# Tokens stored by partition and ids worked out behind the routing, in an attention kernel with expert routing

## Chip, cores and metric

The kernel runs on one core of one Trainium2 chip. The metric is device time in microseconds of one execution. The three runs of the kernel before took 408.19, 408.69 and 409.09 us, median 408.69 us.

## The reference

Attention with pairs of queries averaged, and then one of eight experts (two matrices with a ReLU between) for each token. The output of the attention, heads side by side, is the `x` of the experts.

```python
# q, k, v: 8 batches, 8 heads, 1152 positions, 64 wide
q_pool = q.reshape(B, H, S // 2, 2, D).mean(axis=3)          # 576 queries
scores = (1 / sqrt(D)) * q_pool @ k.T
attn = exp(scores - max) / (sum + 1e-09)
x = (attn @ v).transpose(0, 2, 1, 3).reshape(4608, 512)      # token = batch * 576 + query
for e in range(8):                                           # w1: 512x1024, w2: 1024x512
    mask = domain_id == e
    out[mask] = relu(x[mask] @ w1[e]) @ w2[e]
```

## The kernel before

**Attention.** The 64 heads go through in 32 pairs, four pairs a batch. Time is cut into steps `t`, 12 a pair, 384 in all (`NST`). Scores (`score`, L613) are made in groups of 504 columns for both heads of a pair, ScalarE takes the exponential of a group (`expo`, L621), and TensorE multiplies it with v (`av`, L633). The product of a head gathers in one PSUM bank, `acc`, of which there is one only. When nine chunks are in it, `evac` (L646, L648) takes the reciprocal of the sums and writes the normalised 64 columns of that head into `xb`, on VectorE; until then TensorE can't begin the next head's product. `xb` holds a batch: 128 partitions, five row groups `i`, 512 columns; two such buffers take turns. Row group 0 has 64 rows of its own, the others 128 each, together 576 queries.

A table written out by hand (`PLAN`) says what TensorE does between two score groups: `A` is a product, `P` a piece of an expert's tile, `K` a filler. TensorE's order does not depend on times.

**Stores and gathers.** `put_x` writes a row group of a finished batch to `x_tok` in DRAM in token order. A token's row depends on the query's place in blocks of 96 (`QP`), so a batch is cut into nine stores of 32 to 96 rows (`CUT`), one row group a step behind the batch's last evacuation (`put`). The stores of the first seven batches stand on SyncE's queue, those of the last take turns on SyncE and GpSimd. `get_x` marks a buffer `xs` on VectorE (L96) and then gathers 128 rows of one expert from `x_tok` on GpSimd (L675). Tiles 0 to 2 of an expert hold only rows of the first 2, 4 and 6 batches, tiles 3 and 4 need all.

**Routing.** While attention runs, VectorE works out, from a list `rq` with a cost for each step, which token goes to which slot of which expert: one-hot tables, counts, a running sum, the slot of each token (`rt_...`). `rt_tok` computes the token number that belongs to each partition and row group. Then numbers are moved into slot order with matmuls (`id_...`): `id_prep` splits token number plus one into two digits, `id_group` and `id_lo` make one-hot tiles, `id_mm` (L474) multiplies five of them at a time, two steps behind the last of them (`mmq`), and `id_end` puts the digits together: `grow` (row of `x_tok`, for the gathers) and `gid` (row of the output, for the scatters). Three more steps (`extra`) follow for slots beyond an expert's room.

**Experts.** 14 tiles are worked off as `P` pieces inside attention; the rest comes behind it, expert by expert: `stage1` (L1073), `turn_tile` (L1092: transposes of a gathered tile), `stage2` (L1120), and a scatter of each finished tile.

## Time and profile before

| | |
|---|---|
| median of three runs | 408.69 us |
| the profiled execution | 407.95 us |
| its span (first to last instruction) | 405.9 us |
| busy: TensorE, ScalarE, VectorE, GpSimd | 381.2, 329.3, 230.2, 182.1 us |
| last exponential ends, last matmul of the experts ends (about) | 306.5, 397.7 us |
| granted TensorE clock | 1.00 in nearly the whole span |

Busy time is the union of an engine's records. Records of one engine may overlap, since an instruction can start before the one ahead of it has left the engine. "xb" or "acc" in a row is the tile that is written, what follows "<-" is read. A number in square brackets at the end of a row is idle time of that engine just before, with what seems to have ended it.

### The profile page before, as it was taken

What the parts mean: (1) busy time and instruction counts of PE and PEld (TensorE: products, weight loads), DVE (VectorE), ACT (ScalarE), POOL (GpSimd) and SP (SyncE); (2) the same over time, 40 slices, a digit from 0 to 9 for tenths busy, and PEclk for the clock granted to TensorE, in tenths of its full rate; (3) what the DMA queues carried; (4) which work ended last, traced back from release to release, by engine and by line L of the source; (5) the groups of instructions that cost most, each with busy time, mean ns of one, the idle gap of its engine ahead of it and who ended that gap; (6) DMA issues with size and microseconds to landing.
All of it is one profiled execution on the core that took longest, in us unless ns stands there. A gap on an engine that the chain in (4) does not pass through costs nothing.

```text
span 405.9 us, 14850 instructions
## 1 busy us (share of the span) xinstructions
PE 381.2 (94%) x6341; PEld 259.5 (64%) x6341; DVE 230.2 (57%) x638; ACT 329.3 (81%) x396; POOL 182.1 (45%) x303
## 2 busy tenths in 40 slices
PE   8889888988999999999999999999999999999992
PEld 5456555655676766766767676776776677765542
DVE  4488789985555666555766575566544235433231
ACT  4999999999999999999999999999993333423220
POOL 4633222321645555043433343743443884772522
PEclk9999999999999999999999999999999999999998
DMA  8999999995999999989878865969993399699902
GB/s 216 210 226 236 225 244 236 228 227 125 188 227 250 263 222 232 241 195 255 192 164 191 173 124 126 245 129 211 131 204 90 96 148 209 198 135 167 253 26 100
DMA packets 52751, 76.70 MB, mean 189 GB/s; under 512 B 12239, under 2 KB 41456, under 8 KB 52674
## 3 DMA queue, kind: packets, MB, share of 16 engines
q0 software_dynamic: 38208, 66.53, 80.6%
q1 hardware_dynamic: 14194, 8.99, 10.7%
q8 instruction: 51, 0.84, 0.9%
q14 instruction: 26, 0.21, 0.2%
q10 hardware_dynamic: 272, 0.13, 0.1%
HBM read 95.20 MB, written 14.68 MB: 271 GB/s over the span
## 4 chain that ended last, share of the span: by engine, by line
PE 72%; ACT 12%; DVE 7%; DMA 3%; issue 3%; SPq 1%; POOL 0%; POOLq 0%; ACTq 0%; DVEq 0%
PE s L613 17%; PE acc L633 16%; ACT er L621 12%; PE op L1120 11%; PE hp L1073 10%; PE px L822 6%; PE px L809 6%; DMA q<-in_q_dram 3%; PE s L579 2%; DVE kq L584 2%; DVE xb L648 1%; DVE qz L589 1%; PE px L788 1%; SPq L664 1%; PE hp L1092 1%
## 5 line engine op out<-in xcount | busy, mean ns | idle before, releaser
L621 ACT ACTIVATE er<-s 128x1008 f16<-128x1008 f32 x330 | 298.2, 1110 | 1.1 <-PE s L613 0.8
L633 PE MATMUL acc<-v,er 128*128 128x65 f16 x2835 | 117.4, 194 | 7.4 <-DVE xb L648 4.4
L633 PEld LDWEIGHTS <-er 128*128 128x128 f16 x2880 | 99.9, 97 | 36.6 <-issue 18.3
L613 PE MATMUL s<-qz,kq 64*128 64x504 f16 (+6 forms) x1152 | 112.6, 286 | 6.2 <-ACT er L621 2.7
L675 POOL DMA_INDIRECT xs<-x_tok,grow x40 | 40.7, 1016 | 87.1 <-issue 19.6
L528 POOL DMA_INDIRECT out_dram<-osb,gid x40 | 41.4, 1035 | 62.4 <-DVE osb L828 32.5
L613 PEld LDWEIGHTS <-kq 64*128 64x128 f16 x1152 | 44.1, 94 | 38.5 <-issue 21.0
L117 POOL DMA_DIRECT2D vs<-in_v_dram x32 | 24.0, 749 | 50.1 <-DVE v L554 16.2
L1120 PE MATMUL op<-w2h,hT 128*128 128x512 f16 (+1 forms) x200 | 45.8, 379 | 0.0
L1073 PEld LDWEIGHTS <-w1h 128*128 128x128 f16 x384 | 32.6, 98 | 12.1 <-issue 0.5
L1126 ACT COPY osb<-op 128x512 f32<-128x512 f32 (+1 forms) x14 | 8.2, 583 | 37.8 <-PE op L1120 37.8
L1073 PE MATMUL hp<-xt,w1h 128*128 128x224 f16 (+3 forms) x352 | 38.6, 268 | 0.2 <-ACT hT L1078 0.2
L1080 DVE TENSOR_SCALAR hT<-hp 128x224 f16<-128x224 f32 (+3 forms) x40 | 19.1, 477 | 33.2 <-PE hp L1073 27.1
L1078 ACT ACTIVATE hT<-hp 128x224 f16<-128x224 f32 (+3 forms) x40 | 17.0, 427 | 21.9 <-PE hp L1073 21.6
L584 DVE COPY kq<-s 128x1152 f16<-128x1152 f16 x31 | 23.4, 756 | 18.2 <-PE s L579 15.3
L1120 PEld LDWEIGHTS <-hT 128*128 128x128 f16 (+1 forms) x200 | 20.1, 105 | 18.9
L646 DVE RECIPROCAL cum<-acc 128x5 f32<-128x5 f32 x47 | 9.0, 192 | 40.9 <-PE acc L633 40.7
L809 PE MATMUL px<-xt,w1h 128*128 128x128 f16 x448 | 30.8, 219 | 0.0
L822 PE MATMUL px<-w2h,h 128*128 128x512 f16 x112 | 30.2, 381 | 0.0
L544 DVE TENSOR_TENSOR qp<-q 96x768 f16<-96x768 f32 x31 | 29.3, 946 | 1.4 <-DMA q<-in_q_dram 1.3
L809 PEld LDWEIGHTS <-w1h 128*128 128x128 f16 x448 | 25.3, 98 | 4.9 <-issue 4.7
L814 DVE TENSOR_SCALAR h<-px 128x512 f16<-128x512 f32 x28 | 19.3, 690 | 15.2 <-PE px L809 15.1
(150 smaller groups left out, 346.1 us busy)
## 6 DMA issues: line engine op xcount, KB each, us to landing
q<-in_q_dram POOLq DMA_DIRECT2D x28, 576.0 KB, 8.1
vs<-in_v_dram POOLq DMA_DIRECT2D x32, 288.0 KB, 6.9
k<-in_k_dram POOLq DMA_DIRECT2D x31, 288.0 KB, 6.7
w1h<-in_moe_w_dram POOLq DMA_DIRECT2D x16, 512.0 KB, 13.2
w2h<-in_moe_w_dram POOLq DMA_DIRECT2D x16, 512.0 KB, 13.0
x_tok<-xb SPq DMA_DIRECT2D x23, 96.0 KB, 5.5
q<-in_q_dram SPq DMA_DIRECT2D x3, 576.0 KB, 5.3
x_tok<-xb SPq DMA_DIRECT2D x23, 64.0 KB, 5.4
```

The costliest lines, as they stand in the source:

```text
L117: nc.gpsimd.dma_start(vs[:, :, :, :], v[b, h : h + 2].rearrange("h (p c) d -> p h c d", p=P))
L528: ins = nc.gpsimd.indirect_dma_start(out=dst[:, :], out_offset=bass.IndirectOffsetOnAxis(ap=ap, axis=0), in_=src, in_offset=None, **kw,)
L544: nc.vector.tensor_tensor(out=qp[0:QP, :, :, :].rearrange("p j h d -> p h j d"), in0=q2[:, :, :, 0:D], in1=q2[:, :, :, D : 2 * D], op=ALU.add,
L584: nc.vector.tensor_copy(kq[p][:, :].rearrange("p (c r k) -> p r c k", c=NC, r=2), mt[:, :, 0 : NC * 64].rearrange("p r (c k) -> p r c k", ...
L613: nc.tensor.matmul(s[:, r, o : o + n], lhsT=kq[p][lo:hi, c * P : (c + 1) * P], rhs=qz[p % 2][lo:hi, q0 : q0 + n], start=True, stop=True,)
L621: nc.scalar.activation(er[:, :, o : o + w], st.pop(k)[:, :, 0:w], AF.Exp, bias=0.0, scale=0.0625)
L633: nc.tensor.matmul(acc[p, h][:, i * (D + 1) : (i + 1) * (D + 1)], lhsT=er[:, h, o : o + P], rhs=v16[p % NV][:, c, h, 0 : D + 1], start=c = ...
L675: nc.gpsimd.indirect_dma_start(out=dst, out_offset=None, in_=x_dram[0 : 1 + nb * Sp, :], in_offset=bass.IndirectOffsetOnAxis(ap=ap, axis=0),)
L809: nc.tensor.matmul(m[:, f % 4, :], lhsT=wts[e][0][:, cc, f * P : (f + 1) * P], rhs=h0["xt"][:, cc, :], start=cc == 0, stop=cc == ND - 1,)
L822: nc.tensor.matmul(h0["o"][:, :], lhsT=h0["h"][:, f, :], rhs=wts[e][1][:, f, :], start=f == 0, stop=f == NF - 1,)
L1073: nc.tensor.matmul(hp_[:, lo : lo + n], lhsT=w1h[:, cc, f * P : (f + 1) * P], rhs=xt[:, cc, lo : lo + n], start=cc == 0, stop=cc == ND - 1,)
L1120: nc.tensor.matmul(op_[0:r, :], lhsT=hT[:, f, i * P : i * P + r], rhs=w2h[:, f, :], start=f == 0, stop=f == NF - 1,)
```

## The change

`x_tok` gets a row for each partition and row group: row 1 + b * 640 + 5 * p + i. A batch of `xb` then lies in DRAM as 128 pieces of 5 KB, one for each partition, and goes out in one store, right behind its last evacuation. Rows 64 to 127 of row group 0 are written too and read by nobody, so `x_tok` has 5121 rows instead of 4609. The last batch goes in two parts: columns 0 to 383 behind pair 30, columns 384 to 511 behind pair 31, each part in two halves of 64 partitions, on SyncE and GpSimd.

The routing moves row numbers instead of token numbers, which are an iota (`row1`), so `rt_tok` goes. `grow` comes out of `id_end` as before. The token number `gid` is worked out from the row behind that, in six steps (`id_tok`), with three divisions with rounding. A gather waits for `id_end` (`ready`) and no longer for the list to be empty. The id matmuls come three steps behind their tiles instead of two. Pieces of a tile that is begun when attention's last step comes are done ahead of the last products, with the ReLU on ScalarE. The path for experts with more tokens than room, and the one for sums out of range, are fitted to the new rows; neither runs on these inputs.

```diff
@@ sizes, tables
+    XB = NQ * P
+    NX = B * XB
-    x_dram = nc.dram_tensor("x_tok", (N + 1, Dm), F16, kind="Internal").ap()
+    x_dram = nc.dram_tensor("x_tok", (NX + 1, Dm), F16, kind="Internal").ap()
-    pos = perm.tile([P, B, NQ], I32, name="pos")
-    nc.gpsimd.iota(pos[:, :, :], pattern=[[0, B], [P, NQ]], base=-64, channel_multiplier=1)
-    nc.gpsimd.iota(pos[:, :, 0:1], pattern=[[0, B], [0, 1]], base=0, channel_multiplier=1)
-    bof = perm.tile([P, B, NQ], I32, name="bof")
-    nc.gpsimd.iota(bof[:, :, :], pattern=[[Sp, B], [0, NQ]], base=0, channel_multiplier=0)
+    row1 = perm.tile([P, B, NQ], I32, name="row1")
+    nc.gpsimd.iota(row1[:, :, :], pattern=[[XB, B], [1, NQ]], base=1, channel_multiplier=NQ)
-    nc.gpsimd.memset(pat[:, :], N)
+    nc.gpsimd.memset(pat[:, :], NX)
@@ the routing
-    def rt_tok(i):
...
-            tk = perm.tile([P, NT], I32, name="tk")
-            tf = tok[:, :, :].rearrange("p b i -> p (b i)")
-            nc.vector.tensor_scalar(
-                out=tk[:, :], in0=tf, scalar1=1.0, scalar2=None, op0=ALU.add
-            )
+            tk = row1[:, :, :].rearrange("p b i -> p (b i)")
@@ id_end and what follows it
         nc.vector.tensor_copy(grow[:, :], va[:, :])
-        vz = perm.tile([P, NH], FP32, name="vz")
+        gst["va"] = va
+
+    MAGIC = 12582912.0
+
+    def floor_of(dst, x, n):
+
         nc.vector.tensor_scalar(
-            out=vz[:, :], in0=va[:, :], scalar1=0.0, scalar2=float(N + 1),
-            op0=ALU.is_equal, op1=ALU.mult,
-        )
-        nc.vector.scalar_tensor_tensor(
-            out=gid[:, :], in0=va[:, :], scalar=-1.0, in1=vz[:, :], op0=ALU.add, op1=ALU.add
-        )
+            out=dst, in0=x, scalar1=1.0 / n, scalar2=0.5 - 0.5 / n, op0=ALU.mult, op1=ALU.subtract
+        )
+        nc.vector.tensor_scalar(out=dst, in0=dst, scalar1=MAGIC, scalar2=None, op0=ALU.add)
+        nc.vector.tensor_scalar(out=dst, in0=dst, scalar1=MAGIC, scalar2=None, op0=ALU.subtract)
+
+    vz, vb, vj, vp = (perm.tile([P, NH], FP32, name=n) for n in ("vz", "vb", "vj", "vp"))
+
+    def token_of(step, dst, r, bt, jt, pt):
+
+        if step == 0:
+            floor_of(bt, r, XB)
+            nc.vector.scalar_tensor_tensor(
+                out=jt, in0=bt, scalar=-float(XB), in1=r, op0=ALU.mult, op1=ALU.add
+            )
+        elif step == 1:
+            floor_of(pt, jt, NQ)
+            nc.vector.scalar_tensor_tensor(
+                out=jt, in0=pt, scalar=-float(NQ), in1=jt, op0=ALU.mult, op1=ALU.add
+            )
+        elif step == 2:
+            nc.vector.scalar_tensor_tensor(
+                out=pt, in0=jt, scalar=float(P), in1=pt, op0=ALU.mult, op1=ALU.add
+            )
+            nc.vector.tensor_scalar(
+                out=jt, in0=jt, scalar1=1.0, scalar2=-float(QO[1]), op0=ALU.is_ge, op1=ALU.mult
+            )
+            nc.vector.tensor_tensor(out=pt, in0=pt, in1=jt, op=ALU.add)
+        elif step == 3:
+            floor_of(jt, pt, QP)
+            nc.vector.tensor_scalar(out=pt, in0=pt, scalar1=float(NJ), scalar2=None, op0=ALU.mult)
+        else:
+            nc.vector.scalar_tensor_tensor(
+                out=pt, in0=bt, scalar=float(Sp), in1=pt, op0=ALU.mult, op1=ALU.add
+            )
+            nc.vector.scalar_tensor_tensor(
+                out=dst, in0=jt, scalar=-float(Sp - 1), in1=pt, op0=ALU.mult, op1=ALU.add
+            )
+
+    def id_tok(step):
+        if step == 0:
+            va = gst["va"]
+            nc.vector.tensor_scalar(
+                out=vz[:, :], in0=va[:, :], scalar1=0.0, scalar2=float(NX + 1),
+                op0=ALU.is_equal, op1=ALU.mult,
+            )
+            nc.vector.scalar_tensor_tensor(
+                out=vz[:, :], in0=va[:, :], scalar=-1.0, in1=vz[:, :], op0=ALU.add, op1=ALU.add
+            )
+        else:
+            token_of(step - 1, gid[:, :], vz[:, :], vb[:, :], vj[:, :], vp[:, :])
@@ stores and gathers
-    def put_x(b, i):
-        kept.append((b, i))
-        for lo, hi in zip(CUT, CUT[1:]):
-            i_, m = (0, lo) if lo < 64 else (1 + (lo - 64) // P, (lo - 64) % P)
-            if i_ == i:
-                j, p0 = divmod(lo, QP)
-                (ends[len(cut) % 2] if b == B - 1 else nc.sync).dma_start(
-                    x_dram[1 : N + 1, :].rearrange("(b p j) c -> b j p c", b=B, j=NJ)[
-                        b, j, p0 : p0 + hi - lo, :
-                    ],
-                    xb[b][m : m + hi - lo, i, :],
-                )
-                if b == B - 1:
-                    cut.append((b, i))
+    kept = []
+
+    def put_x(b, lo=0, hi=Dm):
+
+        rows = x_dram[1 + b * XB : 1 + (b + 1) * XB, lo:hi].rearrange("(p i) c -> p i c", i=NQ)
+        if b == B - 1:
+            for eng, p0 in ((nc.sync, 0), (nc.gpsimd, P // 2)):
+                eng.dma_start(rows[p0 : p0 + P // 2], xb[b][p0 : p0 + P // 2, :, lo:hi])
+        else:
+            nc.sync.dma_start(rows, xb[b][:, :, lo:hi])
+        if hi == Dm:
+            kept.append(b)
 
     def gather(dst, ap, nb=B):
         nc.gpsimd.memset(gap[:, :], 0.0)
         nc.gpsimd.indirect_dma_start(
-            out=dst, out_offset=None, in_=x_dram[0 : 1 + nb * Sp, :],
+            out=dst, out_offset=None, in_=x_dram[0 : 1 + nb * XB, :],
             in_offset=bass.IndirectOffsetOnAxis(ap=ap, axis=0),
         )
@@ up
-            if f % 4 == 3:
+            if f % 4 == 3 and now[0] >= NST:
+                nc.scalar.activation(h0["h"][:, f - 3 : f + 1, :], m[:, :, :], AF.Relu)
+            elif f % 4 == 3:
                 nc.vector.tensor_scalar(
                     out=h0["h"][:, f - 3 : f + 1, :], in0=m[:, :, :],
                     scalar1=0.0, scalar2=None, op0=ALU.max,
@@ product
+    CL = 2 * (HP - 1) * D
         if c == NC - 1:
             evac(p, h)
             if p % HP == HP - 1 and h == 1:
-                for i in range(NQ):
-                    if p < NPAIR - 1:
-                        put[t + 1 + i] = (p // HP, i)
-                    else:
-                        put_x(p // HP, i)
+                put_x(p // HP, 0 if p < NPAIR - 1 else CL)
+            if p == NPAIR - 2 and h == 1:
+                put_x(B - 1, 0, CL)
@@ lists
-    rq += [(330, lambda i=i: rt_tok(i)) for i in range(4)]
-            mmq.append((now[0] + 2, c - GL + 1))
+            mmq.append((now[0] + 3, c - GL + 1))
-    extra = [(330, lambda: rt_over(0)), (500, lambda: rt_over(1)), (330, lambda: rt_d(1))]
+    extra = [(330, lambda i=i: id_tok(i)) for i in range(6)]
+    extra += [(330, lambda: rt_over(0)), (500, lambda: rt_over(1)), (330, lambda: rt_d(1))]
@@ main loop
+            for _ in range(len(cur) or len(blocks[0]) if started() else 0):
+                piece()
             for h, c in lead + [(0, 7), (1, 7), (0, 8), (1, 8)]:
                 product(t, (NPAIR - 1, h, c), LAST if h else ACC)
-            while cur or blocks and len(begun) and len(blocks) % 4:
+            while started():
                 piece()
-        if main and want and t >= want[0][2] and t >= last_get + 5 and not (t in later) and not mmq and not rq:
+        if main and want and t >= want[0][2] and t >= last_get + 5 and not (t in later) and ready:
                 id_mm(mmq.pop(0)[1])
                 if not rq and not mmq:
                     id_end()
+                    ready.append(t)
                     rq, extra = extra, []
-        if t in put:
-            put_x(*put.pop(t))
```

**VectorE**, between the evacuations of pair 7, head 1, and of pair 8, head 0 (`rr` and `cum` hold reciprocals, `qp`, `v`, `kp` are the inputs of later pairs, `ov`, `ovi`, `ext`, `oaddr` belong to the routing's end). Before, from the first evacuation to the second:

```order
L648 TENSOR_TENSOR xb<-acc,rr_184 128x5x64
L324 TENSOR_SCALAR ovi<-ov 1x8
L327 TENSOR_SCALAR ovi<-ovi 1x8
L330 TENSOR_REDUCE ovm<-ov 128x1
L544 TENSOR_TENSOR qp_98<-q_1708 96x2x6x64
L349 TENSOR_SCALAR ext<-ext 128x40
L353 TENSOR_TENSOR ext<-ext,isov 128x40
L354 TENSOR_SCALAR oaddr<-ext 128x40
L554 COPY v_1_101<-vs 128x2x9x64
L560 COPY kp<-k_1719 128x2x9x64
L646 RECIPROCAL cum<-acc 128x5
L648 TENSOR_TENSOR xb<-acc,cum 128x5x64
```

After, from the first evacuation on:

```order
L656 TENSOR_TENSOR xb<-acc,rr_181 128x5x64
L458 TENSOR_SCALAR vj<-vp 128x40
L461 TENSOR_SCALAR vj<-vj 128x40
L462 TENSOR_SCALAR vj<-vj 128x40
L488 TENSOR_SCALAR vp<-vp 128x40
L552 TENSOR_TENSOR qp_98<-q_1706 96x2x6x64
L490 SCALAR_TENSOR_TENSOR vp<-vb,vp 128x40
L493 SCALAR_TENSOR_TENSOR gid<-vj,vp 128x40
L562 COPY v_1_101<-vs 128x2x9x64
L314 TENSOR_TENSOR ov<-xf,dl_177 128x8
L317 TENSOR_SCALAR ov<-ov 128x8
L321 TENSOR_TENSOR padr<-ov,padb 128x8
```

Behind these the copy of `kp`, three operations of `ovi` and `ovm` and three of `ext` and `oaddr` still stand ahead of the reciprocal of pair 8; six operations of `id_tok` and three of `ov` have come in between.

**VectorE**, behind the evacuation of pair 5, head 1 (`h` and `osb` are the one-hot tiles that the id matmuls read, `xt` a table they are made from). Before:

```order
L648 TENSOR_TENSOR xb<-acc,rr_184 128x5x64
L452 TENSOR_TENSOR h_1534<-xt_1532,dig 128x10x40
L464 TENSOR_SCALAR osb_1607<-iol,lof 128x128 x5
L464 TENSOR_SCALAR osb_1613<-iol,lof 128x128
L544 TENSOR_TENSOR qp_98<-q_1239 96x2x6x64
L464 TENSOR_SCALAR osb_1613<-iol,lof 128x128 x3
```

After:

```order
L656 TENSOR_TENSOR xb<-acc,rr_181 128x5x64
L423 TENSOR_SCALAR osb_1531<-iol,lof 128x128
L404 TENSOR_TENSOR xt_1600<-hif,iol 128x400
L441 TENSOR_TENSOR dsum<-px,dsum 128x80
L411 TENSOR_TENSOR h_1602<-xt_1600,dig 128x10x40
L552 TENSOR_TENSOR qp_98<-q_1228 96x2x6x64
```

The group of id matmuls that TensorE reaches here used to read the five `osb` of this place; now it reads tiles of which the last is made right behind the evacuation.

**GpSimd**, at the end of attention (`gap` is a marker ahead of each gather). Before:

```order
L675 DMA xs<-x_tok,grow 128x512
L664 DMA x_tok<-xb 32x512
L664 DMA x_tok<-xb 96x512
L664 DMA x_tok<-xb 64x512
L664 DMA x_tok<-xb 32x512
L674 MEMSET gap 1x1
L675 DMA xs<-x_tok,grow 128x512
```

After:

```order
L669 DMA x_tok<-xb 320x1x384
L676 MEMSET gap 1x1
L677 DMA xs<-x_tok,grow 128x512
L676 MEMSET gap 1x1
L677 DMA xs<-x_tok,grow 128x512
L669 DMA x_tok<-xb 320x1x128
L676 MEMSET gap 1x1
L677 DMA xs<-x_tok,grow 128x512
```

Four stores behind the last evacuation have become one, and one more stands two gathers ahead of it.

## Rows read from the trace of the kernel before

**Rows 1.** Stretch, length; busy PE, PEld, DVE, ACT, POOL (instructions); clock, DMA share, GB/s.

```profile
100.00:306.40 206.40, 202.82 (x4032) 144.10 (x4032) 121.24 (x291) 206.40 (x230) 94.23 (x144) 1.00 0.94 196
308.10:397.70 89.60, 89.41 (x647) 56.75 (x645) 31.83 (x86) 28.04 (x60) 52.31 (x96) 1.00 0.81 151
```

**Rows 2.** TensorE's waits, 8-100, 100-306.4, 306.4-400 us: us in total, times, longest.

```profile
PE acc L633 <- DVE xb L648: 3.6, 7, 1.0
...
PE acc L633 <- DVE xb L648: 0.8, 1, 0.8
...
PE hp L1073 <- ACT hT L1078: 0.2, 1, 0.2
```

**Rows 3.** VectorE in order of time, 88 to 94 us: start, length, what.

```profile
88.45 0.16 DVE L315 TENSOR_TENSOR ov<-xf,dl 128x8 f32<-128x8 f32 x1
88.64 0.17 DVE L318 TENSOR_SCALAR ov<-ov 128x8 f32<-128x8 f32 x1
...
89.33 0.49 DVE L648 TENSOR_TENSOR xb<-acc,rr 128x320 f16<-128x320 f32 x1
...
91.84 0.45 DVE L560 COPY kp<-k 128x1152 f16<-128x1152 f16 x1
93.45 0.20 DVE L646 RECIPROCAL cum<-acc 128x5 f32<-128x5 f32 x1 [1.16 <-PE acc L633]
93.84 0.49 DVE L648 TENSOR_TENSOR xb<-acc,cum 128x320 f16<-128x320 f32 x1 [0.20 <-DMA x_tok<-xb]
```

**Rows 4.** TensorE and ScalarE in time; ScalarE's group; the chain near 93 us.

```profile
94.39 0.63 PE L633 MATMUL acc<-v,er 128*128 128x65 f16 x15 [0.98 <-DVE xb L648]
...
156.14 14.55 ACT L621 ACTIVATE er<-s 128x1008 f16<-128x1008 f32 x16
...
L621 ACT ACTIVATE er<-s 128x1008 f16<-128x1008 f32 x330 | 298.2, 1110 | 1.1 <-PE s L613 0.8
...
93.31 2.12 ACT er L621 x2
...
95.44 0.61 ACT er L621
```

**Rows 5.** VectorE in order of time: small operations of 128x40.

```profile
51.28 0.17 DVE L372 TENSOR_SCALAR jj<-jj 128x40 f32<-128x40 f32 x1
51.49 0.18 DVE L375 TENSOR_SCALAR jj<-jj 128x40 f32<-128x40 f32 x1
...
53.39 0.17 DVE L341 TENSOR_SCALAR isov<-slot 128x40 f32<-128x40 f32 x1
53.48 0.19 DVE L344 SCALAR_TENSOR_TENSOR ext<-dal,slot 128x40 f32<-128x40 f32 x1
```

**Rows 6.** Around id matmuls in order of time, two places; ScalarE at the first.

```profile
70.55 0.86 PE L474 MATMUL px<-h,osb 128*128 128x80 f16 x5 [0.17 <-DVE osb L464]
...
85.21 0.34 PE L474 MATMUL px<-h,osb 128*128 128x80 f16 x5
...
70.43 2.41 ACT L621 ACTIVATE er<-s 128x1008 f16<-128x1008 f32 x2
```

**Rows 7.** Instructions on `x_tok`: stores on SyncE, ns; landing of stores and gathers.

```profile
L664 SPq DMA_DIRECT2D x_tok<-xb x68: 322/472/1325, 51.4 to 311.6; - x68
...
DMA to landing us min/median/max: 2.3/5.8/8.0
```

**Rows 8.** The last stores, gathers, transposes in order of time.

```profile
309.38 2.76 SPq L664 DMA_DIRECT2D x_tok<-xb  x5
309.65 2.17 POOL L664 DMA_DIRECT2D x_tok<-xb  x4 [0.88 <-DVE xs L96]
...
314.64 1.00 POOL L675 DMA_INDIRECT xs<-x_tok,grow  x1 [2.78 <-DVE hT L1080]
...
315.95 0.95 POOL L675 DMA_INDIRECT xs<-x_tok,grow  x1 [0.23 <-issue]
...
320.95 0.63 PE L1092 MATMUL hp<-ident,xs 128*128 128x128 f16 x8
```

66 lines of the change are left out of this document (24 added, 42 removed).

## Prediction

> **What bounds the kernel now.** I read the page first, then the busy time by stage, then what TensorE waits for in each stage, and last the places that the change touches. The table by stage [rows 1] shows two programs, one after the other. Up to 306.4 us ScalarE is the bound: its exponentials fill 206.40 of 206.40 us between 100 and 306.4, while TensorE is busy for 202.82 of them. Two records of ScalarE may overlap, so "busy" hides small losses; sixteen exponentials in a row without a disturbance take 14.55 us at 1.11 us each [rows 4], so one starts every (14.55 - 1.11)/15 = 0.90 us. Behind 308.1 us TensorE alone is the bound: 89.41 of 89.60 us busy, and the one wait in it is 0.2 us on ScalarE [rows 1, 2]. So nothing that a store or a gather does can shorten that part, unless TensorE's own work gets less, and the change leaves every matmul in the program; it can only add a wait. What is left to win is what ScalarE loses while it waits for scores, and these waits come from TensorE waiting for VectorE: for the evacuation of an accumulator (`xb`, L648) 3.6 us in 7 places up to 100 us, 0.8 us in one place behind it [rows 2].
>
> **The stores.** Removed are 72 stores of 32 to 96 rows, added 7 stores of a whole batch and 4 halves. On SyncE an issue took 0.32 to 1.33 us, a landing 2.3 to 8.0 us [rows 7]. SyncE computes nothing, and of its queue only the three early transposes of x stand among these stores; they feed the run at 308 us, which has no wait. The bytes go from 576 to 640 rows a batch; a 5 KB piece has no row in this trace, so a batch's store may land sooner than nine small ones or later than 8.0 us. Nobody waits for either: a buffer of x is written again only when the batch between has gone by, and the gathers that need a batch stand on GpSimd, for which TensorE never waits [rows 2]. I put 0 on it, from both sides. Two iotas less on GpSimd at the start stand ahead of no load that is late: 0.
>
> **Fewer semaphores.** The first evacuation of batches 2 to 7 waits for the landing of what the buffer held: eight DMA semaphores before, one now. It shows as an idle time of 0.20 us between reciprocal and multiply [rows 3]; the multiply at 89.33 has none. VectorE is on the path there, so the pause goes: -0.2 us at 93.8 us. At the five other batch starts TensorE hardly waits for `xb` (one wait of 0.8 us in the whole stretch behind 100 us [rows 2]), so between 0 and -0.1 us each; I take -0.1 us in all.
>
> **The last batch.** Six of its eight heads are now stored behind pair 30, the rest behind pair 31, and each store has a half on SyncE and a half on GpSimd. Before, the five issues on SyncE lasted from 309.38 to 312.14 us, and the first gather behind them started at 314.64, the second at 315.95; TensorE transposes their tiles at 320.95 without an idle time [rows 8]. One issue each instead of five and four frees that gather some 2 us sooner. No gain: TensorE is full. GpSimd now has a store that waits for the evacuation of pair 30, head 1, and behind it stand two gathers and then the last store. They were waiting for VectorE there anyway, so 0.
>
> What speaks against the change is the length of the pieces: 768 and 256 bytes instead of 1 KB. The Trainium skill (DMA: Bandwidth & Descriptors, Specifications) wants at least 512 bytes for full rate and says that shorter transfers are done by read-modify-write. No row here times a store of 256 bytes. By that rule the last gather would start later, not sooner; the sum stays as it is until the delay uses up the room ahead of 320.95, which is the third rival.
>
> **The routing, earlier.** Taken out are eight small operations on VectorE (`posf`, `jj`, `tok`, `tk`; one starts 0.21 us behind another that it needs [rows 5]), so all that follows comes some four steps sooner, and the id matmuls now come three steps behind their one-hot tiles instead of two. Before, the five id matmuls at 70.55 us stretched to 0.86 us since VectorE was still at their operands; five that find theirs ready took 0.34 us [rows 6]. ScalarE shows the price: two exponentials in 2.41 us there, a spacing of 1.30 where 0.90 is normal, 0.4 us lost. In the new order (the second place shown with the change) the tile needed there is done right behind the evacuation. So this loss should go; whether it stays gone is the next term.
>
> **The token ids, later.** Seventeen more operations of 128x40 now stand behind the id matmuls. Gathers now wait for the row numbers alone, not for the rest of the routing's list; the first is due at step 112 in both, when either is done. The first scatter that wants an id comes with the first tile's end, long behind them. On VectorE the place that matters is between the evacuations of pair 7, head 1 (ends 89.33 + 0.49 = 89.82 us) and of pair 8, head 0 (its reciprocal starts at 93.45, when the accumulator is done). Before, the work in between lasted to 91.84 + 0.45 = 92.29, that is 2.47 us, and then VectorE had 1.16 us to spare [rows 3]. Now nine more operations stand in it: four of `id_tok(4)`, two of `id_tok(5)` and the three of `ov` that stood ahead of the first evacuation. At 0.21 us where one needs the one before [rows 5] and 0.19 for the `ov` ones [rows 3], with one that needs nothing at 0.1 (53.39 to 53.48 [rows 5]), that is 5 x 0.21 + 0.1 + 3 x 0.19 = 1.72 us: 0.6 us more than the room. The reciprocal comes 0.6 us late, the pause of 0.2 us is gone, so the accumulator is free 0.4 us later than before. This place has no cover. TensorE already waits there, to 94.39, with one accumulator for all products, and ScalarE already starves: two exponentials from 93.31 to 95.44, 0.3 us more than twice 0.90 [rows 4]. So +0.4 us. And since VectorE's queue, not TensorE, then sets the time, what was won at 70 us is waited out here: if TensorE arrives 0.4 us sooner, it waits 0.4 us more. That is why I do not add the two.
>
> Between 100 us and the end the built program is the same on TensorE and ScalarE, row for row; the new Relu on ScalarE and the pieces at step NST are not in it, since no piece is begun there. **Sum** against the profiled execution (span 405.9, time 407.95 us): +0.4 (evacuation of pair 8) - 0.1 (other batch starts) + 0 (stores, tail, 70 us) = +0.3 us, 408.2. The median of the runs shown is 0.74 us above that execution, so I forecast 408.69 + 0.3 = **409.0 us**.
>
> **The rivals.**
> 1. Nothing is handed on: ScalarE has score buffers ahead at 94 us, and the 0.4 us goes into them. For it speaks that the 0.98 us of TensorE's wait cost ScalarE only 0.3; against it, that what is added to a starved place is paid in full. 408.7 us.
> 2. Faster: the ids fit into VectorE's spare 1.16 us (operations at 0.1 us instead of 0.21), so 0.4 us at 70 us is kept, the 0.3 at 95 us goes too, and 0.1 to 0.2 at the batch starts: -0.9 us, 407.8. Against it speaks the spacing of each chain in [rows 5].
> 3. Slower, by the last store: its 256-byte pieces take 8.0 us to land (the longest of [rows 7]) instead of some 2 us. Then the first gather starts near 309.4 + 0.5 (an issue) + 8.0 = 317.9, the second 1.3 us behind it, as before [rows 8], at 319.2, and with a landing of 2.3 to 3.3 us its tile is there at 321.5 to 322.5 instead of before 320.95: about 1.1 us of waiting in a part that has no slack, 409.8 to 410.2 us. It decides from a landing of about 7 us. Against it: nothing near 312 us in [rows 8] took so long, the pieces then were four times as large, and a whole store of nine was through in 5.3 us.
> 4. Slower, by VectorE's queue in more than one place: eleven more operations ahead of pair 7's evacuation against seven one-hot tiles, a sum and the three `ov` that have left (+0.3 us), a stretched group of id matmuls that only moves from 70 us to the next evacuation instead of going (+0.4), and the 0.4 us of pair 8 on top: +1.1, 409.8 us.
>
> **How the numbers follow.** This kernel can be told from no change by about 0.2%, 0.8 us. Forecast 0.48, rival 1 0.17, rival 2 0.17, rival 3 0.06, rival 4 0.12. Forecast and rival 1 are within 0.2%. Rival 2 lies at the edge, 0.13 of it faster and 0.04 the same; rivals 3 and 4 are slower, 0.18. So faster 0.13, same 0.69, slower 0.18. The range reaches from rival 2 (407.8) to rival 4 (409.8, with 0.2 for the scatter of the runs, 408.2 to 409.1); outside are part of rival 3 and the tails of 2 and 4, under 0.2.
>
> **What would show it.** Right: no other wait of TensorE behind 308 us; about 94.0 us for the reciprocal of pair 8, with VectorE full from 89 us on and no idle time ahead of it; the id matmuls near 70 us at 0.34 us; the first gather of x at once behind its marker on VectorE. Wrong: idle time on VectorE ahead of that reciprocal (rival 2), a wait on the gathers of x at 320 us (rival 3), a late evacuation of pair 7 (rival 4), or any change in the spacing of the exponentials behind 100 us, which none of the terms touches.

## The result, and the profile after

The changed kernel took 411.63 us (three runs, 411.24 to 412.01) against 408.69 us before: ratio 1.0063, 95% interval 1.0036 to 1.0089. It is slower by 2.9 us, 0.4 to 0.9%, where 409.0 us (407.8 to 410.0) was forecast. The profiled execution is the longest of the three: 412.01 us, span 410.0 against 405.9.

Three stretches first (columns as in [rows 1]; the last but two is the granted clock of TensorE). The kernel before has 1.00 in all three.

```profile
63.00:74.00 11.00, 8.89 (x159) 5.96 (x160) 8.06 (x27) 9.65 (x11) 2.85 (x4) 0.84 1.15 228
92.00:104.00 12.00, 9.91 (x186) 7.04 (x186) 7.82 (x30) 10.56 (x13) 3.25 (x4) 0.86 0.63 143
...
310.00:400.00 90.00, 89.82 (x697) 57.50 (x695) 32.17 (x87) 28.86 (x63) 50.39 (x93) 1.00 0.71 148
```

Twice on the way the clock was at the lower of its two levels, 1.2 instead of 2.4 GHz: from 66.08 to 69.50 and from 96.80 to 100.22 us. Behind 310 us TensorE is as full as it was [rows 1]. What TensorE waited for (us in total, times, longest). The first row is the kernel before from 7 to 105 us ([rows 2] begin at 8 and end at 100), the others are the changed kernel from 7 to 105 us, from 105 to 200 and from 308 on:

```profile
PE acc L633 <- DVE xb L648: 4.4, 8, 1.0
...
PE acc L641 <- DVE xb L656: 4.1, 8, 1.1
...
PE px L853 <- DVE dsum L441: 1.9, 2, 1.5
...
PE px L433 <- DVE dsum L441: 0.3, 1, 0.3
...
PE px L790 <- issue: 0.8, 1, 0.8
...
PE hp L1078 <- ACT hT L1083: 0.2, 1, 0.2
```

The waits for `xb` have not grown in sum. New are three waits of `px` for `dsum`, two of them of fillers (L853), and one for nothing that the trace names ("issue"). The first place, TensorE in order of time:

```profile
63.05 0.34 PE L433 MATMUL px<-h,osb 128*128 128x80 f16 x5
63.33 0.39 PE L621 MATMUL s<-qz,kq 64*128 64x432 f16 x4
65.19 0.41 PE L853 MATMUL px<-warm 128*128 128x288 f16 x2 [1.48 <-DVE dsum L441]
...
67.31 1.83 PE L641 MATMUL acc<-v,er 128*128 128x65 f16 x30
```

L433 is a group of five id matmuls, L853 a pair of filler matmuls (`zeros`, a K of the plan). Both write the one `px` buffer of `xps`, so the filler may not start before VectorE has read the group's sums. VectorE in the same stretch:

```profile
62.72 0.45 DVE L562 COPY v<-vs 128x1152 f16<-128x1152 f16 x1
63.09 0.56 DVE L404 TENSOR_TENSOR xt<-hif,iol 128x400 f16<-128x400 f32 x1
63.58 0.45 DVE L568 COPY kp<-k 128x1152 f16<-128x1152 f16 x1
63.94 1.05 DVE L411 TENSOR_TENSOR h<-xt,dig 128x400 f16<-128x400 f16 x2
64.92 0.23 DVE L441 TENSOR_TENSOR dsum<-px,dsum 128x80 f32<-128x80 f32 x1
66.46 0.19 DVE L654 RECIPROCAL rr<-acc 128x5 f32<-128x5 f32 x1 [1.32 <-PE acc L641]
```

The group was done near 63.4 us, but its sum stands behind 1.5 us of other work, and the filler, which computes nothing, holds up all of TensorE until 65.19. In the kernel before this filler stood ahead of the group and did not wait:

```profile
63.21 0.42 PE L846 MATMUL px<-warm 128*128 128x288 f16 x2
...
64.63 0.34 PE L474 MATMUL px<-h,osb 128*128 128x80 f16 x5
```

Then the clock fell: 30 products took 1.83 us, and VectorE had to wait 1.32 us in its turn. ScalarE shows the price:

```profile
66.02 2.95 ACT L629 ACTIVATE er<-s 128x1008 f16<-128x1008 f32 x3 [0.39 <-PE s L621]
69.75 1.91 ACT L629 ACTIVATE er<-s 128x1008 f16<-128x1008 f32 x2 [0.78 <-PE s L621]
```

[rows 6] had a group of id matmuls stretched to 0.86 us, at 70.55 us. Here the groups at 70.70 and 72.86 us take 0.34 us, and it is the next one that waits in its middle for a one-hot tile and lasts from 75.75 to 76.60 us:

```profile
75.75 0.27 PE L433 MATMUL px<-h,osb 128*128 128x80 f16 x3
76.23 0.37 PE L433 MATMUL px<-h,osb 128*128 128x80 f16 x2 [0.20 <-DVE osb L423]
```

The second place answers [rows 3] and the first row of [rows 4]. VectorE, then TensorE:

```profile
95.71 0.20 DVE L352 TENSOR_TENSOR ext<-ext,isov 128x40 f32<-128x40 f32 x1
95.94 0.18 DVE L353 TENSOR_SCALAR oaddr<-ext 128x40 int32<-128x40 f32 x1
96.04 0.18 DVE L654 RECIPROCAL cum<-acc 128x5 f32<-128x5 f32 x1
96.26 0.49 DVE L656 TENSOR_TENSOR xb<-acc,cum 128x320 f16<-128x320 f32 x1
```

```profile
96.81 1.01 PE L641 MATMUL acc<-v,er 128*128 128x65 f16 x15 [1.14 <-DVE xb L656]
```

As forecast, the reciprocal of pair 8 starts with no idle time behind the routing's operations, and the pause of 0.20 us ahead of the multiply is gone. (It is gone at all six batch starts: the kernel before has 0.20 or 0.21 us between reciprocal and multiply at each, the changed kernel 0.03 or 0.04, as at every other evacuation.) TensorE waits 1.14 us instead of 0.98; but 15 products then take 1.01 us instead of 0.63, since the clock is at half.

The stores answer [rows 7] and [rows 8]: 0.33 us to issue a batch. Of the eleven stores the trace shows five landings: three whole batches in 7.4, 9.6 and 7.4 us, and of the last batch the two halves on SyncE, in 4.4 us (pieces of 768 bytes) and 2.3 us (pieces of 256 bytes, issued at 313.96 us). In [rows 7] the median of 5.8 and the 8.0 us count gathers too; the stores alone took 2.3 to 7.5 us there. Nobody on the path waits for a landing.

```profile
L671 SPq DMA_DIRECT2D x_tok<-xb x7: 332/332/367, 51.6 to 279.6; - x7
...
DMA to landing us min/median/max: 2.3/7.4/9.6
```

GpSimd, the first gather behind it (it waits for its marker on VectorE, not for a store):

```profile
317.57 0.98 POOL L677 DMA_INDIRECT xs<-x_tok,grow  x1 [2.59 <-DVE xs L98]
```

**Where the 4.1 us of span came from.** Both programs run the same 330 exponentials, so I set the start of each against its start in the kernel before. The first 60 add 0.26 us; up to number 75 (the first place) come 1.53; to 84, 0.27 (0.17 of it by number 77, right behind the stretched group); to 94, 0.29 (a second filler behind an id group, 0.46 us at 86.80); to 104 (the second place) 1.51; to 136, 0.26; to 146 (the pause) 0.72; to the last one -0.26. Behind it the end comes 0.5 us sooner, nearly all of that behind the last matmul; why, was not studied. Sum 4.1.

### The profile page after: what moved, and what is told of

Read it like the earlier page. It is cut to its first block, busy times and chain, and to the rows that moved or that the text cites. A ratio compares the mean times of both kernels' runs of the same rounds, so it can differ in the third digit from the quotient of the medians.

```text
span 410.0 us, 14758 instructions
## 1 busy us (share of the span) xinstructions
PE 382.1 (93%) x6341; PEld 260.7 (64%) x6341; DVE 232.3 (57%) x647; ACT 330.5 (81%) x396; POOL 181.2 (44%) x299
## 4 chain that ended last, share of the span: by engine, by line
PE 75%; DVE 11%; ACT 7%; DMA 3%; issue 2%; POOL 0%; POOLq 0%; SPq 0%; DVEq 0%; ACTq 0%
PE acc L641 18%; PE s L621 18%; PE op L1125 11%; PE hp L1078 10%; ACT er L629 7%; PE px L826 7%; PE px L811 6%; PE s L587 3%; DMA q<-in_q_dram 3%; DVE kq L592 2%; DVE xb L656 2%; DVE qz L597 1%; PE px L790 1%; DVE qp L552 1%; PE hp L1097 1%
## 5 line engine op out<-in xcount | busy, mean ns | idle before, releaser
L641 PE MATMUL acc<-v,er 128*128 128x65 f16 x2835 | 118.9, 195 | 7.4 <-DVE xb L656 4.9
L641 PEld LDWEIGHTS <-er 128*128 128x128 f16 x2880 | 101.3, 98 | 36.8 <-issue 18.9
```

The costliest lines, as they stand in the source:

```text
L641: nc.tensor.matmul(acc[p, h][:, i * (D + 1) : (i + 1) * (D + 1)], lhsT=er[:, h, o : o + P], rhs=v16[p % NV][:, c, h, 0 : D + 1], start=c = ...
```

## The experiments

On the chips of these runs every kernel, the one before too, took 428 to 433 us: from exponential 200 on all are late, and the runs of one kernel spread by 2%. Two copies of the kernel before measured 1.0044 (0.9999 to 1.0088) and 1.0005 (0.9971 to 1.0039) against itself. So ratios resolve some 0.4%. Up to exponential 120 the profiles agree well: the two copies are within 0.06 us of the first profile. So the table goes by that: how much later than before an exponential starts, less the same at number 60. (Up to there executions lie 0.6 us ahead to 0.3 us behind, but both_back 2.4 us: it has a wait of 1.49 us at 14.19 us, and behind it the clock at half from 16.12 to 19.53.) Waits and clock are from each profile.

| profile | filler's wait, 65 us | clock 63-74 | exp 75 | wait for pair 8 | clock 92-104 | exp 104 | exp 120 |
|---|---|---|---|---|---|---|---|
| before_again | - | 1.00 | 0.00 | 0.99 | 1.00 | 0.00 | 0.00 |
| before_third | - | 1.00 | 0.05 | 0.98 | 1.00 | 0.05 | 0.05 |
| after | 1.48 | 0.84 | 1.53 | 1.14 | 0.86 | 3.60 | 3.60 |
| changed_again | 1.48 | 1.00 | 0.43 | 1.14 | 1.00 | 1.05 | 1.06 |
| changed_third | 1.49 | 0.84 | 1.66 | 1.15 | 0.86 | 3.24 | 3.24 |
| changed_fourth | 1.48 | 0.84 | 1.54 | 1.14 | 0.86 | 3.62 | 3.62 |
| id_groups_back | - | 1.00 | 0.00 | 2.38 | 0.86 | 2.02 | 2.02 |
| filler_first | - | 1.00 | -0.36 | 0.90 | 1.00 | 0.24 | 0.23 |
| ids_late | 1.48 | 0.84 | 1.38 | 0.82 | 1.00 | 1.72 | 5.25 |
| both_back | - | 1.00 | 0.13 | 0.81 | 1.00 | -0.03 | 1.99 |
| first_filler | - | 1.00 | -0.36 | 1.15 | 0.86 | 1.71 | 1.71 |
| first_filler_spread | - | 1.00 | -0.36 | 1.15 | 1.00 | 0.30 | 0.30 |
| three_moves | - | 1.00 | -0.36 | 0.82 | 1.00 | -0.27 | -0.27 |

The five other profiles of kernels with the three moves show the same: no filler's wait, -0.25 to -0.36, 0.81 to 0.86, 1.00 and -0.27.

**The id groups where they stood.** My theory was the filler at 65 us and the token ids ahead of pair 8; rivals were the stores, and one place as the sequel of the other.

```
+    rq += [(330, lambda: None)] * 4
-            mmq.append((now[0] + 3, c - GL + 1))
+            mmq.append((now[0] + 2, c - GL + 1))
```

> The changed kernel with the identity-matmul groups of the routing put back on the score groups where the kernel before had them: four empty entries stand in the routing list where the removed token steps stood, and a group is released two steps behind its last compare again, not three. Everything else of the change stays, the token-id chain ahead of pair 8's evacuation too. Theory: the change lost its time at two places of the attention stage, each a TensorE wait followed by 3.4 us at the half clock. The first, at 65 us, arises because an identity group now comes ahead of the filler matmuls that need the same single px buffer, so the filler waits 1.48 us for dsum; with the groups back that wait, the half clock behind it and the smaller wait at 86.8 us are gone. Exp 70 then stands within 0.3 us of the kernel before (1.79 us late in the changed kernel), and the whole takes 409.4 us (411.6 less 1.8 and 0.4). Rival one, the stores of a whole batch disturb the cores' other traffic: nothing here touches them, 411.6. Rival two, the second half-clock stretch at 97 us is a sequel of the first: both go, 408.0.

The filler's wait and the first half-clock stretch are gone, exponential 75 is level. But the id chain moved with the groups and now stands wholly ahead of pair 8:

```profile
95.88 0.63 PE L641 MATMUL acc<-v,er 128*128 128x65 f16 x15 [2.38 <-DVE ovi L323]
```

2.0 us are lost there, though nothing was lost ahead of it. So a loss at the second place needs none at the first, and the stores are not the cause of the first. My forecast had not seen this longer wait. Ratio 0.9985 (0.9944 to 1.0026).

**The filler first.** In the plan, `A2 K2/A2` became `A2K2 -/A2`, and `A4 K2/A2` became `A4K2 -/A2`: each pair of fillers half a window sooner, ahead of its group.

> The changed kernel with two pairs of filler matmuls moved half a score window ahead, so that each stands in front of the identity group that it stood behind (groups 61 and 83); the identity groups keep the places that the change gave them. Theory: the order of filler and identity group in the one px buffer is what costs at 65 and 86.8 us, not the earlier place of the groups itself; so the 1.48 us and 0.46 us waits for dsum go, and the time is 409.4 us as with the groups put back. Rival: the earlier groups delay VectorE's other work there whatever the filler does; then a TensorE wait of a similar size shows at another instruction between 63 and 75 us, exp 70 stays 1.5 us or more late, and the time stays at 411.2 to 411.8.

```profile
62.65 0.41 PE L853 MATMUL px<-warm 128*128 128x288 f16 x2
63.11 0.34 PE L433 MATMUL px<-h,osb 128*128 128x80 f16 x5
```

The wait for `dsum` is gone, the groups stay where the change put them, and exponential 75 is even 0.36 us ahead: the loss at 70 us [rows 6] is what went. So it is the order of filler and group in one buffer. The pair moved to 83 loses 0.8 us up to number 84 (where it stays, 0.3, and 0.3 more by number 94 at its own wait); and the wait for pair 8 is 0.90 with the clock at full speed, which I had not expected. Ratio 0.9973 (0.9939 to 1.0007).

**The token ids late.**

```
-    extra = [(330, lambda i=i: id_tok(i)) for i in range(6)]
+    toks = dict(zip((115, 116, 117, 120, 122, 123), range(6)))
...
+        if t in toks:
+            id_tok(toks.pop(t))
```

> The changed kernel with the six steps of the token-id chain taken out of the routing list and put at steps 115, 116, 117, 120, 122 and 123, behind both evacuations of pair 8 (their result is first needed by a scatter behind step 129). Theory: the second loss, at 96 to 101 us, comes from the chain standing ahead of pair 8's first reciprocal on VectorE; with it gone the wait of TensorE for that evacuation falls from 1.14 us to 0.9 or less, the clock stays at full speed there, and the steps between exp 90 and exp 100 add 0.4 us or less against the kernel before instead of 1.5; 410.1 us in all. The first loss at 65 to 74 us stays. Rival one: the clock falls at that place whatever VectorE does (as a sequel of the first fall): 411.4. Rival two: the chain only moves the pile, and pair 9's first evacuation is late in place of pair 8's: 411 or more, with a new TensorE wait near 107 us.

The wait for pair 8 falls to 0.82 us and nothing is lost there, but the second rival holds: the chain, some of its operations at 0.43 to 0.51 us instead of 0.18, makes pair 9 late.

```profile
106.14 0.46 PE L641 MATMUL acc<-v,er 128*128 128x65 f16 x5 [1.99 <-DVE xb L656]
```

And the stretch from 104 to 112 us, columns as above:

```profile
104.00:112.00 8.00, 6.01 (x97) 4.45 (x94) 4.51 (x18) 5.48 (x7) 0.80 (x2) 0.59 1.15 222
```

The clock falls again, and 3.3 us are lost by number 112. Ratio 1.0057 (1.0019 to 1.0095).

**Both edits.**

> Both edits at once: identity groups on the score groups of the kernel before, and the token-id chain behind pair 8's evacuations. Theory: the two losses add, so 411.6 less 2.2 less 1.5 is 407.9 us, a little under the kernel before (408.7), whose own waits for pieces of the stores this kernel does not have; an open 0.8 us is the pause of TensorE at 139 us between two transposes of the changed kernel, for which no semaphore is the cause: if the stores cause it, it is here again and the time is 408.7. Rival, the stores are the cost: 410.5 or more.

Nothing is lost up to number 104, then 2.0 us at pair 9 (a wait of 1.57 us, clock 0.79 from 104 to 112). The sum I expected fails by that one place. Ratio 1.0039 (1.0002 to 1.0076).

**The changed kernel again, and the kernel before.** No edit.

> The changed kernel, unaltered, beside the others of this call. In the runs of the call before, the three kernels in which an identity group stood ahead of its filler or was put back lost their time at other places, so each place must be seen twice on one chip. Theory: the 1.48 us wait of the filler for dsum near 65 us, 3.4 us at the half clock behind it, a wait of 1.0 to 1.2 us ahead of pair 8's evacuation with a second half-clock stretch, and a pause of 0.4 to 1.1 us between two transposes near 139 us come again; 411.6 us, or 2.9 us more than the kernel before on whatever chip. Rival: the second stretch and the pause are accidents of one run; then exp 146 stands 2.5 us or less behind the kernel before (4.6 us in the first run, counted from exp 60).

The rival holds for the clock: the same two waits to 0.01 us, and no fall behind either. The same stretches as above, in this profile:

```profile
63.00:74.00 11.00, 8.68 (x181) 5.75 (x177) 9.16 (x31) 10.54 (x12) 2.85 (x4) 1.00 1.15 238
92.00:104.00 12.00, 9.85 (x191) 6.28 (x187) 6.94 (x27) 11.82 (x14) 5.02 (x7) 1.00 0.61 138
```

By number 120 it has lost 1.06 us instead of 3.60. The pause is there: 0.77 us. Ratio 1.0039 (1.0009 to 1.0068).

> The kernel before, unaltered, for its profile on the chip of this call: 408.7 us if the chip is like the first, and the profile shows whether a pause without a semaphore between two matmuls near 137 to 140 us belongs to this chip or to the changed kernel. Theory: none there over 0.2 us. Rival: 0.4 us or more there too.

No pause without a semaphore near 139 us and no fall there, but 0.6 us for `qz` at 135.28, which the first profile has at 0.17; on these chips the kernel before loses 0.5 to 0.8 us from number 136 to 146 too.

**The first filler alone, and with the stores in quarters.** In the plan only the pair of group 62 moved; in the second kernel also

```
-            nc.sync.dma_start(rows, xb[b][:, :, lo:hi])
+            for j in range(4):
+                parts[now[0] + 1 + j] = (b, rows[32 * j : 32 * j + 32], ...)
```

> The changed kernel with only the first of the two moved pairs of filler matmuls: the pair at score group 62 stands ahead of the identity group of group 61; the pair at 84 stays where it is. With both moved, the loss at 65 us was gone, but exp 84 still came 0.8 us later than the steps before it, and the half-clock stretch at 97 us was gone too although the token-id chain still filled VectorE ahead of pair 8's reciprocal. Theory: the second stretch is a sequel, TensorE reaches the wait for pair 8 earlier than VectorE is ready only because the first loss has left the two out of step; so here too there is none, and exps 104 to 120 stand 0.2 to 0.6 us behind the kernel before (0.3 us from the wait at 84). Rival: the moved pair at 84 is what removed it; then the wait ahead of pair 8 is 1.1 us or more again and 1.5 us are lost at 97 us. Time by the theory 409.7 us, the pause at 139 us included.

> As the kernel with only the first pair of fillers moved, and the store of each whole batch (all but the last) put out in four stores of 32 partitions, one a step, in place of one of 128; the pieces in DRAM are 5 KB as before. Theory: the pause of TensorE near 139 us, which nothing but its own instruction stream ends, comes because a packet of instructions waits behind 655 KB of one store in the DMA engines; with a quarter at a time it is 0.2 us or less and the time is 0.8 us lower, 408.9 us. Rival: the pause has to do with where the instruction stream stands (a boundary of a packet at these transposes) and not with the store; then it is 0.4 us or more again.

These are the same program around pair 8, with the same wait of 1.15 us. In one the clock fell behind it (exponential 104 at 1.71), in the other it did not (0.30). So the second stretch is no sequel of the first, and my theory that it is falls; behind the same wait the clock falls in one execution and not in the other. The pause is 0.93 and 0.80 us: quarters do not remove it. Ratios 0.9942 (0.991 to 0.9974) and 0.9962 (0.993 to 0.9994).

**Three moves.** First filler as above; the pair of group 84 half a window later (`-/A2K2`); the last two id steps at steps 115 and 116.

```
-    extra = [(330, lambda i=i: id_tok(i)) for i in range(6)]
+    toks = {115: 4, 116: 5}
+    extra = [(330, lambda i=i: id_tok(i)) for i in range(4)]
```

> The changed kernel with three moves and nothing left out: the filler pair of score group 62 ahead of the identity group of group 61, the filler pair of group 84 half a window later (behind it VectorE has read the px buffer), and the last two of the six token-id steps at steps 115 and 116, behind both evacuations of pair 8. Theory, from the two profiles each of the changed kernel and of the kernel with the first filler moved: the direct price of the three TensorE waits is 0.45, 0.3 and 0.1 us, and the rest of the loss (1.3 us at each of two places) comes only in those executions in which the granted clock falls to half behind them. Without the waits neither comes: TensorE waits for pair 8 for 0.8 to 1.0 us as in the kernel before (1.14 now), the clock stays at 1.0 from 60 to 130 us, and exp 120 stands within 0.2 us of the kernel before, counted from exp 60. Time 2 us or more below the changed kernel of the same call. Rival: the chain's last steps delay pair 9's first evacuation as the late chain did (1.99 us of waiting); then exp 112 is 0.5 us or more late.

> The kernel with the three moves, once more, as the control for the two others. Theory: the pause between the third and fourth transpose (at 135.4 us in its first profile, 1.06 us) comes again with 0.4 us or more, as in every profile so far of a kernel that stores batch 2 in one piece (0.45 to 1.1 us) but for the two of three_moves_store_late. Rival: it comes and goes from one execution to the next, here too.

```profile
94.20 0.63 PE L641 MATMUL acc<-v,er 128*128 128x65 f16 x15 [0.82 <-DVE xb L656]
```

What was expected of the places came: no wait for the sum by a filler, 0.82 us for pair 8, clock 1.00, and 0.27 us ahead of the kernel before by number 120. The whole did not: 2 us or more below the changed kernel were forecast, and on the same chip the medians are 430.8 against 431.8 us (changed_third), runs of either spreading over 4 to 6 us. Ratios to the kernel before 0.9948 (0.9912 to 0.9984) and 0.9953 (0.9918 to 0.9988). The pause was 1.06 us in the first profile, 0.33 in the second. All eight runs with the first filler moved alone or with the three moves, whatever their stores, lie between 0.9927 and 0.9965 of the kernel before, on four chips.

> The changed kernel a third time, as the measure for the two others on the same chip and as a third look at the clock behind the same two waits (1.48 us at 65 us and 1.14 us at 96 us): it fell behind both in the first profile and behind neither in the second. Theory: the waits are the same to 0.02 us, and the exps lose 0.4 to 0.5 us at the first place and 0.1 us at the second where the clock stays, 1.3 to 1.8 us and 1.5 us where it falls. Rival: a wait of the same length costs the same whatever the clock.

> The changed kernel once more, for the whole time and for the clock behind its two waits. Theory: waits of 1.48 and 1.14 us again; by the three profiles so far the clock falls behind the first in some executions and behind the second in some, and exp 120 stands 1.0 us (no fall), 2.2 to 2.5 us (one fall) or 3.3 to 3.6 us (two) behind the kernel before, counted from exp 60. Against the kernel before the whole is 1.0 to 4.0 us longer on a chip where the stages from 200 us on run as in the first profiles; where all kernels take 5% more, the difference drowns. Rival: with the waits as they are the loss by exp 120 is some other value.

Both falls in both, waits as before; loss by number 120 3.24 and 3.62 us. (0.9965, 0.9929 to 1.0001, and 0.9999, 0.9961 to 1.0037: on these two chips the changed kernel is not slower than the one before, by the whole. One reason can be read from the profiles: from number 120 to the last exponential the two copies of the kernel before fall behind its first profile by 10.3 and 9.4 us, the 15 profiles of kernels with the change's layout on these chips by 6.6 to 8.5. On the two chips that have both, that is 1.8 to 2.9 us less; in its first profile the change won nothing there (0.7 us lost). What does it was not tried.)

> The kernel before a third time, as a measure for the two others: exps from 60 to 130 us as in its two profiles to 0.05 us, waits for pair 8 of 0.98 us with the clock at 1.0 behind them, no pause without a semaphore near 139 us. Rival: the clock falls there in this kernel too.

As expected: 0.98 us, clock 1.00, no such pause.

**The pause at 139 us.** In the first profile, TensorE and what ended the idle time:

```profile
137.90 0.34 PE L790 MATMUL px<-ident,xs 128*128 128x128 f16 x3
139.05 0.23 PE L790 MATMUL px<-ident,xs 128*128 128x128 f16 x1 [0.81 <-issue]
```

Four transposes of one tile, and a gap between the third and the fourth. It is always at the same matmul of the program, and it always ends 1.2 to 1.5 us behind the end of a packet of 16 KB on the queue of instructions:

```profile
q8 instruction: 51, 0.84, 0.8%
```

The Trainium skill (Advanced Engine Details and Errata, ISA Cache) gives the line of the instruction cache as 16 KB, 256 instructions. The trace agrees: 51 packets of 16 KB, that is 13,056 instructions at 256 each, stand against 12,720 recorded ones of TensorE. So, it seems, TensorE ran out of instructions. What makes the packet late?

```
+            if b == 2:
+                parts[now[0] + 10] = (b, rows, xb[b][:, :, lo:hi])
+                return
```

> The same with the store of batch 2 (the one in flight at 139 us) put out ten steps later, some 9 us. In every run so far TensorE paused without a semaphore at the same matmul of the program, the fourth transpose of the second x tile, for 0.45 to 1.1 us, 1.3 to 1.4 us behind the end of a 16 KB packet of instructions; both profiles of the kernel before have none there. Theory: that packet is late because the store of batch 2 is in the DMA engines then; with the store later the packet starts 1 us or more earlier against the exps, and the pause is under 0.2 us. Exp 146 against exp 136: 0.0 to 0.3 us behind the kernel before (0.5 to 0.9 us otherwise). Rival: the packet's time hangs on something else; the pause stays.

> The kernel with the three moves and the store of batch 2 ten steps later, once more. Theory: no fall of the clock between 60 and 130 us, exp 120 0.2 to 0.3 us ahead of the kernel before and no pause near 139 us, as in its first profile; with the 0.5 us that the last stores gave behind the attention stage, the whole is 0.5 to 1.0 us below the kernel before and 2 to 4 us below the changed kernel on an undisturbed chip. Rival: the earlier ratio of 0.993 came from the disturbed chip, and this kernel is level with the kernel before or slower.

The pause was 0.17 and 0.02 us. But the edit did nothing: SyncE has no other work in between and issued the store at 127.25 us, as in three_moves (127.69). So these two say only that the pause varies with the execution. Ratios 0.9927 (0.9888 to 0.9966) and 0.9941 (0.9909 to 0.9973). Then the store went to GpSimd, twenty steps later (`nc.gpsimd.dma_start` in the above), and, in another kernel, each batch in pieces of 1 KB:

```
-            nc.sync.dma_start(rows, xb[b][:, :, lo:hi])
+            for i in range(NQ):
+                nc.sync.dma_start(rows[:, i, :], xb[b][:, i, lo:hi])
```

> The same with the store of batch 2 issued by GpSimd twenty steps later. In three_moves_store_late the store did not start later at all: SyncE has nothing between the two places in its queue and issued it at 127.25 us as in three_moves (127.69), and the two programs are otherwise the same row for row; so what it showed of the store says nothing. GpSimd's queue stands behind a gather that starts at 137 us, so here the store starts behind the place of the pause. Theory: the packet of instructions is late because of the store; without it in flight the pause is 0.2 us or less, and the packet that started at 133.2 us (9.1 us behind the one before it) starts 1 us earlier. Rival: the pause is 0.4 us or more with the store not yet issued; then the stores have nothing to do with it.

> The same as three_moves, every whole batch stored in five stores of 128 rows of 1 KB, all put out at once, in place of one of 5 KB pieces; the rows stand in DRAM where the change puts them. Theory of the piece size: the packet of instructions waits behind 5 KB pieces, and with 1 KB pieces, as in the kernel before, the pause is 0.2 us or less. Rival: the bytes in flight count, not the pieces; the pause stays at 0.4 us or more.

```profile
134.83 0.23 PE L799 MATMUL px<-ident,xs 128*128 128x128 f16 x1 [0.71 <-issue]
...
140.20 0.56 POOL L681 DMA_DIRECT2D x_tok<-xb  x1
```

With the store of batch 2 not yet issued the pause is 0.71 us: that store is not needed for it. With 1 KB pieces there is none, as in the three profiles of the kernel before. In before's time the packet starts at 131.2 to 131.7 us in those four; in the 15 others at 132.2 to 133.3, with a pause of 0.33 to 1.1 us in 13 of them. The later this packet ends, the longer the pause: where it ends at 133.3 to 133.6 (in before's time) the pause is 0.02 to 0.45 us, at 133.6 to 134.1 it is 0.6 to 1.0, and at 134.3, 1.06 and 1.11. That the packet is late, and the pause follows, is seen; why it is late, stays open: one kernel with 1 KB pieces is one profile. What it costs on these chips is small, since without it 0.5 us are lost there anyway (`qz`, as in before_again). Ratios 0.9947 (0.9912 to 0.9982) and 0.9965 (0.993 to 1.0001).

## Why the prediction was wrong

- **The routing, earlier: the step that failed.** I saw that the id matmuls move and asked only whether their operands are ready. I did not ask what else takes turns in the buffer that they write, and so put the term at 0. The filler behind them waits 1.48 us for a sum at the end of VectorE's queue, and a second one 0.46 us. From changed_again and three_moves, without a fall of the clock: 0.43 + 0.36 = 0.8 us at the first, 0.3 at the second. Another 0.3 us goes between number 75 and 84 in every kernel with the groups at their new places, and not in id_groups_back (0.00 to -0.01); some 0.15 of it comes right behind the group at 75.75 us, which now stretches in place of the one at 70 us. The loss at 70 us did go (0.36). It was not waited out at pair 8 either: first_filler_spread gets there 0.76 us ahead of changed_again (0.23 against 0.99 at number 94) and waits the same 1.15 us, since VectorE's queue is ahead by as much; three_moves keeps 0.27 to number 120.
- **The clock was in no term.** It was at 1.00 in the kernel before until 402 us, and I treated a wait as worth its length. Behind a wait of 1.48 us it fell in four of five profiles, behind 1.14 or 1.15 us in four of six, behind 1.57, 1.99 and 2.38 us each time, at the evacuations of pairs 8 and 9 with 0.81 to 0.99 us in none, nor behind the pauses of up to 1.11 us at 139 us. A fall added 1.0 to 1.2 us at the first place (1.38 to 1.66 against 0.43), and 1.0 to 1.5 at the second. What decides between two executions with the same wait, no run here shows. The Trainium skill (TensorE: Matmul & The Clock Gate, Part 1) says of the rise at the start of matmul work that its moment varies from run to run. Four profiles of one program, three with both falls and one with none, show as much of a fall: not only its moment, but whether it comes.
- **The token ids, later.** Mechanism and place were right: VectorE full, the reciprocal without idle time. The size was off. The reciprocal came at 96.04, which is 93.69 in before's time (less the 2.35 us by which exponential 94 is late): 0.24 us late, not 0.6, since the work ahead of it grew by 1.40 us, not 1.72. With the pause gone the multiply began 0.07 us late, not 0.4; TensorE waited 0.16 us longer, and without a fall exponential 104 lost 0.06 us against the kernel before; with one, 1.0 to 1.5.
- **Fewer semaphores.** Right: the pause of 0.20 us is gone at all six batch starts. In store_of_1k_pieces, where the wait is for five stores instead of eight or one, it is 0.08 us at each.
- **Stores and last batch, 0.** No engine on the path waited for one, as said, though whole batches land later (7.4 to 9.6 us); the first gather behind the last store came some 1.7 us sooner against the exponentials, and nothing was won by it. Rival 3 is refuted by a landing of 2.3 us for 256-byte pieces; its 8.0 us was a gather's. The Trainium skill's rule on 512 bytes (DMA: Bandwidth & Descriptors, Specifications) shows no harm here. Whether the stores have a part in the pause at 139 us, or in the 2 to 3 us won behind number 120 on the later chips, is open.
- **"Between 100 us and the end the same".** The rows are the same, the time is not: the pause at 139 us costs 0.7 us. Its cause is not settled.
- **The rivals.** Rival 4 (VectorE's queue in several places, +1.1 us) came nearest in sign. Of its places the stretched group did move to the next evacuation, for some 0.15 us instead of 0.4; the evacuation of pair 7 came 0.04 us late instead of 0.3; pair 8 cost 0.06 instead of 0.4. Neither the filler's buffer nor the clock was in it. That its +1.1 equals what is lost by number 120 without a fall (1.06) is luck.
- **What does not add up.** Without falls the places sum to 1.1 us by number 120, with both to 3.6. The other two runs of the first measurement were not profiled; one had a mean clock of 0.994, which leaves no room for two falls (each takes 3.41 x 0.5 / 410 = 0.004), and still took 411.63 us. So some of its 2.9 us is unexplained. And on the later chips the whole shows no certain loss: 1.0039 of the kernel before (on a chip where its copy measured 1.0044), 0.9965 and 0.9999. Why all kernels are 5% longer there was not looked into; all their profiles, of the kernel before too, have the clock at half for 3 to 14 us between 330 and 370 us, which the two profiles of the first measurement do not.

## What to carry to other kernels

When a group of instructions moves, list everything that shares its output buffer and now stands behind it, work that computes nothing too: a filler meant to keep TensorE busy stopped it. Ask of each new wait not only how long it is but whether TensorE idles longer than it ever did before, since the granted clock can fall behind it and more than double its price (0.43 us became 1.4 to 1.7). And a chain that is moved off one evacuation needs a place with idle time behind it, or the next evacuation pays (1.99 us of waiting in ids_late): split in two, it cost nothing here.

## What the runs showed of the hardware

The same wait of TensorE, to 0.01 us, was followed by half the clock in some executions and not in others. TensorE paused at one fixed instruction, for 0.02 to 1.11 us in 15 profiles, the longer the later a 16 KB packet on the queue of instructions ended (133.3 to 134.3 us in before's time); that it had run out of instructions fits this and is not shown. A multiply on VectorE that has to wait for eight stores, all landed long before, starts 0.20 or 0.21 us behind the reciprocal's end at all six places; with five stores it is 0.08, with one 0.03 or 0.04. Four TENSOR_SCALAR operations of 128x40 on VectorE took 0.43 to 0.51 us instead of 0.18 in a stretch in which GpSimd issued transfers without a break (ids_late, 99.5 to 103.5 us); that the one causes the other was not tried.
